# Plain rows for w1 and w2, short packets for w_out, dummy products in the opening, and one later load

## The chip, the cores and the metric

The kernel runs on one core of a Trainium2 chip. The metric is the device time of one execution in microseconds (us). Engines are named as in the profile: PE is TensorE (products; PEld its weight loads), DVE is VectorE, ACT is ScalarE, POOL is GpSimd, SP issues DMAs.

## The reference

Eight sequences of 4160 rows of 192 values go through a dynamic convolution and then through a feed-forward layer with a maximum of two products:

```python
w = softmax(weight_gen)                      # over 7 taps, for 8 heads of 24 channels
out = np.einsum('bshk,bskhg->bshg', w, x_unf)  # x_unf: the row and the 6 before it
x = out.reshape(33280, 192)
h1 = x @ w1                                  # 192 -> 1024
h2 = x @ w2
return np.maximum(h1, h2) @ w_out            # 1024 -> 192
```

The kernel takes `max(h1, h2)` as `h1 + relu(h2 - h1)`. With `wd = w2 - w1` and `w10 = w1 @ w_out`, the result is `y @ w10 + relu(y @ wd) @ w_out`, where y is what the convolution gives. `wd` and `w10` are made on the chip at the start of every execution.

## The kernel before

**Tiling.** Partition p holds 260 neighbouring rows of the flattened input; a column is one row of each partition. Columns are worked on in batches of 16 (`BATCHES`), and these in units of 4 columns (the first two batches) or 8. For each unit VectorE multiplies x with the softmax weights (`mul`, L211); in the first two batches TensorE sums the seven taps while it transposes (`sum_transpose`, L281) and ScalarE copies the result out (`sums_out`, L293); later VectorE adds (L227 to L236) and a DMA transposes (`transpose`, L245). TensorE then makes the hidden features with `wd` (`hid_tile`, L336), ScalarE applies the relu (L346), and TensorE makes the results: `out_first` (L387, with `w10`) and `out_hidden` (L375, with `wo`). ScalarE copies these out (`evac`, L431) and SP stores them.

**Features.** A chunk f of the 1024 features is 128 of them. `load_wo` (L577) gives partition p, for each half of the features, four neighbouring rows of w_out, 3072 B in one piece. So chunk f of `wo` holds every fourth row of its half, and `features` (L588) reads the columns of w1 and w2 in the same order, one in four. Everything that makes `wd` and `w1` reads through `features`: three differences on VectorE (`diff`, L593: d.0, d.1, d.2) and three casts on ScalarE (`cast_w1`, L611: c.0, c.1, c.2). TensorE turns each difference by half its rows (`turn`, L601: t.0 to t.2), and ScalarE copies the turned ones into `wd` (`turn_out`, L607: T.0 for two of them, T.1 for the third). The first features need T.0. `w1` is transposed by products (`w1_products`, L628: v.0) and multiplied with `wo` (`w10_product`, L647: p.0).

**Order.** The start is written out by hand: `OPENING` is a list of steps, and each engine does its share of them in that order. `k.n` makes n dummy products of 512 columns (`keep_warm`, L663), whose output nobody reads. `h` and `r` are a tile of features and its relu; `y` and `e` the sums and their copy; `m` a product of VectorE; `X`, `n`, `l`, `s`, `W` the steps of the softmax, with `W.b.o` the weights of batch b from column o on; `A`, `B`, `D`, `E` the results of a group; `xa` and `xv` the casts of the first x. Loads are `lx` (x), `lg` (weights of the convolution), `lw` and `lt` (w1 and w2), `lo` (w_out), `lh` (the rows before a batch). The name behind an `@` is the step whose instruction the load waits for. `lw` and `lt` are issued by SP; `lo` and `lx` by POOL, which writes them as bf16; POOL issues its loads in the order of the list. Behind the opening, groups of features follow in a loop (L772).

Of the kernel before, what the change touches and what calls it, by code (L numbers as in the profile page):

```python
# [17 lines left out]
def _sub(base: bass.AP, off: int, dims):  # L18
    ap = [list(base.ap[0])] + [[int(s), int(c)] for s, c in dims]
    return dataclasses.replace(base, offset=base.offset + off, ap=ap)  # L20
# [3 lines left out]
def kernel(  # L24
# [11 lines left out]
    B, S, D = x.shape  # L36
    H, K = weight_gen.shape[2], weight_gen.shape[3]
    F = moe_w1.shape[1]
    P = 128
    PAD = K - 1  # L40
    WGC = H * K
    FCH = F // P
    HF = F // 2
# [421 lines left out]
    OUTS, c = [[], [], []], 0  # L465
    for g in range(3, len(GROUPS)):
        most = 4 if g == 3 else 2 if GROUPS[g][1] == 2 or len(OUTS[-1]) == 4 else 4
        n = min(most, ready[g] - c)
# [67 lines left out]
    wo = consts.tile([P, FCH * D], BF16, name="wo")  # L536
# [11 lines left out]
    ws = {(kind, wi): stage.tile([P, w], FP32, name=f"ws{wi}{kind}") for kind, w in (("E", F), ("T", HF)) for wi in range(2)}  # L548
# [26 lines left out]
    def load_wo(_=None):  # L575

        return nc.gpsimd.dma_start(  # L577
            out=wo[:, :].rearrange("p (h e) -> p h e", h=2),
            in_=bass.AP(tensor=moe_w_out.tensor, offset=0, ap=[[4 * D, P], [HF * D, 2], [1, 4 * D]]),
        )  # L580

    def block(i):
# [2 lines left out]

    def features(i, wi):

        return _sub(ws["T", wi] if i == 2 else ws["E", wi], i % 2 * HF, [[1, 4], [4, P]])  # L588

    def diff(i):  # L590

        a, b = (features(i, wi) for wi in (1, 0))
        return nc.vector.tensor_tensor(out=block(i), in0=a, in1=b, op=ALU.subtract)  # L593
# [15 lines left out]
    def cast_w1(i):  # L609

        return nc.scalar.copy(out=w1[:, i * HF:(i + 1) * HF], in_=features(i, 0))  # L611
# [79 lines left out]
    def results_buffer(_):  # L691
# [5 lines left out]
    DO = {  # L697
        "Z": results_buffer,
        "xf": lambda c0, n: load_x_first(c0, n), "lw": load_w, "lt": load_last, "lo": load_wo,
        "lg": lambda b, i=0, of=1: load_wg(b, nc.sync if b < 2 else nc.gpsimd, i, of), "lx": load_x, "lh": load_halo,  # L700
        "xv": lambda c0, n: cast_x("v", c0, n), "xa": lambda c0, n: cast_x("a", c0, n),
# [6 lines left out]
    }  # L708

    OPENING = """  # L710
        lg.0 xf.-6.6 xf.0.4 lt.1.1 lt.0.0 lw.0.1 lw.0.0 lt.1.0 k.1 lw.1.1 lt.0.1 lw.1.0 lg.1 X.0.0.2 X.0.1.2 n.0.0.2 n.0.1.2 l.0.0.2 l.0.1.2 s.0.0.2 W.0.0.0 s.0.1.2 xa.-6.4 W.0.0.1 W.0.8 xv.-2.6 k.19 lx.0.4.4@l.0.0.2 lx.0.12.4@W.0.8 m.0.0.0 c.0 W.0.12 k.1 m.0.0.1 W.0.4 y.0.0 y.0.1 e.0.0 c.2 d.0 d.2 e.0.1 t.0 c.1 t.2 T.0 d.1 t.1 T.1 m.0.4 lx.0.8.4@W.0.4 lo.0@e.0.0 lg.3@e.0.1 h.0 X.1 r.0 h.1 r.1 lx.1.0.8@m.0.4 v.0 n.1 l.1 V.0 h.2 y.1 r.2 e.1 m.0.8 s.1 lg.2@r.2 m.0.12 h.3 r.3 h.4 h.5 V.1 r.4 W.1.0 W.1.4 m.1.0 y.2 r.5 e.2 h.6 lx.1.8.8@W.1.0 m.1.4 p.0 C.2 h.7 y.3 C.1 lh.2 C.0 r.6 r.7 X.2 n.2 W.1.8 A.3 m.1.8 e.3 B.3 h.8 D.3 r.8 Z.0 E.3 A.4 B.4 lx.2.0.8.0@r.8 h.9 l.2 X.3 W.1.12 y.4 e.4 r.9 s.2 D.4 h.10 E.4 W.2.0 n.3 r.10 lg.4@r.10 A.5 y.5 h.11 e.5 l.3 m.1.12 B.5 r.11 D.5 h.12 E.5 A.6 B.6 h.13 D.6 r.12 y.6 E.6 lx.2.8.8 r.13 A.7 e.6 h.14 h.15 W.2.8 B.7 r.14 r.15 D.7 y.7 E.7 e.7
    """

    make_identity(nc, ident_f)
# [91 lines left out]
```

## Time and profile before

| | |
|---|---|
| median of 3 runs | 413.85 us (412.47 to 414.23) |
| the profiled execution | 411.03 us, of which the span of instructions is 409.2 us |
| PE busy | 395.3 us (97%), 7492 products and as many weight loads |
| DVE, ACT, POOL busy | 370.6 us (91%), 362.6 us (89%), 66.2 us (16%) |
| mean granted clock of TensorE | 0.995 |
| DMA | 63.16 MB in 59,251 packets |

Busy times are shares of the span. "Idle before" is what an engine stood still ahead of an instruction, and the name behind the arrow is what ended it; "issue" means that nothing in the profile ended it. The granted clock is the share of TensorE's full clock. In the rows on DMA, q0 is the queue that POOL issues to, q1 that of SP, and q8 one that fetches instructions. Times in the text count from the start of the span.

### The profile page before, as it was taken

How to read it: one execution, taken by the hardware profiler on the slowest of the kernel's cores; microseconds unless marked ns; L12 is line 12 of the kernel's file. 1: busy time of each engine (PE TensorE's matmuls, PEld its weight loads, DVE VectorE, ACT ScalarE, POOL GpSimd, SP SyncE). 2: the span in 40 equal slices, each digit the busy share in tenths (PEclk: the TensorE clock that was granted, in tenths of full speed). 3: DMA queues.
4: the chain of work that ended last, by engine and by line, in shares of the span. 5: the costliest groups of instructions: out<-in, count | busy, mean ns of one | idle time of the engine just before them, and what ended most of it. 6: DMA issues, size and time to landing. Idle time of an engine off the chain costs nothing.

```text
span 409.2 us, 16299 instructions
## 1 busy us (share of the span) xinstructions
PE 395.3 (97%) x7492; PEld 320.0 (78%) x7492; DVE 370.6 (91%) x211; ACT 362.6 (89%) x465; POOL 66.2 (16%) x96
## 2 busy tenths in 40 slices
PE   6699699999999999999999999999999999999996
PEld 2489699777777777777778777877778777787995
DVE  6999969999999999999999999999999999998200
ACT  5999599999999998899998999989999899888872
POOL 2211020112111112121211122120022221201000
PEclk9899999999999999999999999999999999999999
DMA  8944548866478763975676577388448747557304
GB/s 270 244 94 110 125 105 216 157 152 153 117 138 184 192 153 90 257 185 84 205 204 99 112 219 200 60 246 184 95 101 232 180 78 198 141 102 189 104 39 158
DMA packets 59251, 63.16 MB, mean 154 GB/s; under 512 B 46521, under 2 KB 47801, under 8 KB 59184
## 3 DMA queue, kind: packets, MB, share of 16 engines
q1 hardware_dynamic: 51952, 40.15, 36.5%
q0 software_dynamic: 7088, 21.89, 26.7%
q8 instruction: 58, 0.95, 0.9%
q10 hardware_dynamic: 144, 0.10, 0.1%
q14 instruction: 9, 0.07, 0.1%
HBM read 36.55 MB, written 25.56 MB: 152 GB/s over the span
## 4 chain that ended last, share of the span: by engine, by line
PE 94%; ACT 2%; DMA 1%; issue 1%; SPq 1%
PE op_ps L375 42%; PE hdc L336 13%; PE hda L336 13%; PE hdb L336 13%; PE op_ps L387 8%; PE hdp L336 3%; PE yps L281 2%; DMA ws0E<-in_moe_w_dram 1%; ACT w L611 1%; ACT yt L293 0%; PE pw L647 0%; PE tp L628 0%; ACT en_t L191 0%; SPq L570 0%; ACT rd_t L346 0%
## 5 line engine op out<-in xcount | busy, mean ns | idle before, releaser
L375 PE MATMUL op_ps<-wo,rd_t 64*128 64x192 bf16 x4160 | 210.4, 243 | 0.0
L375 PEld LDWEIGHTS <-rd_t 64*128 64x128 bf16 x4160 | 180.6, 94 | 14.9
L211 DVE TENSOR_TENSOR m_t<-xb,en_t 128x10752 bf16<-128x10752 bf16 (+2 forms) x39 | 187.7, 4818 | 3.4 <-ACT en_t L191 2.4
L336 PEld LDWEIGHTS <-wd 64*128 64x128 bf16 x1824 | 95.9, 95 | 41.2 <-issue 1.6
L346 ACT ACTIVATE rd_t<-hdc 128x1024 bf16<-128x1024 f32 x82 | 84.1, 1025 | 18.1 <-PE hdc L336 16.4
L346 ACT ACTIVATE rd_t<-hdb 128x1024 bf16<-128x1024 f32 x81 | 83.5, 1030 | 0.0
L346 ACT ACTIVATE rd_t<-hda 128x1024 bf16<-128x1024 f32 x81 | 83.4, 1029 | 0.0
L253 POOL CAST gate<-yt 128x1 f32<-128x1 bf16 x30 | 33.8, 1128 | 284.5 <-DMA yt<-y_t 284.5
L227 DVE TENSOR_TENSOR m_t<-m_t 128x4608 bf16<-128x4608 bf16 (+1 forms) x30 | 72.9, 2429 | 0.1
L336 PE MATMUL hdc<-yt,wd 64*128 64x512 bf16 (+1 forms) x552 | 67.8, 353 | 0.0
L431 ACT COPY o_t<-op_ps 128x384 f32<-128x384 f32 (+1 forms) x99 | 56.0, 576 | 12.6 <-PE op_ps L375 12.6
L336 PE MATMUL hda<-yt,wd 64*128 64x512 bf16 (+1 forms) x540 | 67.0, 355 | 0.0
L336 PE MATMUL hdb<-yt,wd 64*128 64x512 bf16 (+1 forms) x540 | 67.0, 355 | 0.0
L387 PE MATMUL op_ps<-w,yt 64*128 64x192 bf16 x780 | 55.4, 243 | 0.0
L387 PEld LDWEIGHTS <-yt 64*128 64x128 bf16 x780 | 38.7, 94 | 14.7 <-issue 0.3
L233 DVE TENSOR_TENSOR m_t<-m_t 128x3072 bf16<-128x3072 bf16 (+1 forms) x30 | 50.1, 1669 | 0.1
L191 ACT ACTIVATE en_t<-wg_t 128x896 bf16<-128x896 f32 (+3 forms) x48 | 35.4, 766 | 2.3 <-PE op_ps L375 2.0
L236 DVE TENSOR_TENSOR y_t<-m_t 128x1536 bf16<-128x1536 bf16 (+1 forms) x30 | 27.4, 913 | 0.5
L168 DVE TENSOR_REDUCE sum_t<-e_t 128x64 f32<-128x448 f32 (+3 forms) x31 | 19.6, 634 | 5.4 <-ACT e_t L153 5.4
L177 DVE TENSOR_TENSOR wg_t<-wg_t,sum_t 128x280 f32<-128x280 f32 (+6 forms) x46 | 22.0, 480 | 0.0
L125 POOL DMA_DIRECT2D xb<-in_x_dram x34 | 18.2, 535 | 18.0 <-ACT en_t L191 8.5
L153 ACT ACTIVATE e_t<-wg_t 128x896 f32<-128x896 f32 (+2 forms) x18 | 15.8, 883 | 2.0 <-DMA wg_t<-in_weight_gen_dram 2.0
(39 smaller groups left out, 111.7 us busy)
## 6 DMA issues: line engine op xcount, KB each, us to landing
out_dram<-o_t SPq DMA_DIRECT2D x27, 768.0 KB, 4.4
xb<-in_x_dram POOLq DMA_DIRECT2D x30, 384.0 KB, 5.5
wg_t<-in_weight_gen_dram POOLq DMA_DIRECT2D x13, 448.0 KB, 6.4
out_dram<-o_t SPq DMA_DIRECT2D x10, 384.0 KB, 4.6
xb<-xb POOLq DMA_DIRECT2D x7, 288.0 KB, 5.0
wg_t<-in_weight_gen_dram SPq DMA_DIRECT2D x2, 448.0 KB, 5.0
xb<-in_x_dram POOLq DMA_DIRECT2D x4, 192.0 KB, 5.3
xs<-in_x_dram SPq DMA_DIRECT2D x1, 576.0 KB, 4.2
```

The costliest lines, as they stand in the source:

```text
L177: nc.vector.tensor_tensor(out=w_t, in0=w_t, in1=_sub(s_ts[b], hs.start, [[1, hs.stop - hs.start], [0, K]]), op=ALU.subtract)
L191: act = nc.scalar.activation(out=_sub(en_ts[b], (o * WGC + ((i or 0) * J + j) * N * K) * 2, [[2 * N, K], [2, N], [1, 2]]), in_=_sub(wg_ts[ ...
L211: return nc.vector.tensor_tensor(out=m_out, in0=x_in, in1=_sub(en_ts[b], at * H * 2, [[2, K * n * H], [0, G // 2], [1, 2]]), op=ALU.mult,)
L227: nc.vector.tensor_tensor(out=taps(0, 1, 3), in0=taps(0, 1, 3), in1=taps(3, 1, 3), op=ALU.add)
L233: nc.vector.tensor_tensor(out=taps(0, 2, 2), in0=taps(0, 2, 2), in1=taps(1, 5, 2), op=ALU.add)
L236: nc.vector.tensor_tensor(out=_sub(y_ts[b], o * D, [[64, 2], [P, 3 * w // 2], [1, 64]]), in0=taps(0, 1, 1), in1=taps(2, 1, 1), op=ALU.add,)
L253: nc.gpsimd.tensor_copy(out=gate, in_=yt[:, 0:1])
L336: nc.tensor.matmul(hid_out(t, f, j), lhsT=wd_at(j, s, f // 4, f % 4 * P, P), rhs=_sub(yt_ts[u][half(j), :], (s + j) % 3 * P, [[3 * P, w // ...
L346: relu_of[t0] = nc.scalar.activation(out=rd[:, k * 1024:(k + n) * 1024], in_=hd[:, at:at + n * 1024], func=AF.Relu)
L375: return nc.tensor.matmul(op_out(c), lhsT=rd[half(r), k * 1024 + at:k * 1024 + at + P], rhs=wo[half(r), f * D:(f + 1) * D], start=False, s ...
L387: nc.tensor.matmul(op_out(c + j), lhsT=yt_ts[u][half(j), (3 * i + (s + j) % 3) * P:(3 * i + (s + j) % 3 + 1) * P], rhs=w10[half(j), s * D: ...
L431: copied = nc.scalar.copy(out=_sub(o, c % 24 * D, [[D, len(qs)], [h * D, 2], [1, D]]), in_=_sub(tile_, at + (qs[0] - p) * D, [[D, len(qs)] ...
```

## The change

`load_wo` now gives partition p one row of each chunk: row p of chunk f is row 128 f + p of w_out, so that a piece is 768 B, and there are 1024 of them instead of 256. `features` then reads a half of the columns of w1 and w2 as they lie. In `OPENING`:

- dummy products: k.1 now stands ahead of W.0.0.0 instead of behind W.0.12; k.3 is new between y.0.0 and y.0.1, k.2 behind t.0, k.4 behind t.2 and k.2 behind t.1;
- the load of the first batch's last four columns, lx.0.12.4, waits for xa.-6.4 instead of W.0.8;
- the load of the third batch's second half, lx.2.8.8, waits for W.2.8 and is issued then; W.2.8 itself moves from behind h.15 to ahead of r.13;
- V.0 stands ahead of l.1, and W.1.8 ahead of r.7.

```diff
     def load_wo(_=None):
 
         return nc.gpsimd.dma_start(
-            out=wo[:, :].rearrange("p (h e) -> p h e", h=2),
-            in_=bass.AP(tensor=moe_w_out.tensor, offset=0, ap=[[4 * D, P], [HF * D, 2], [1, 4 * D]]),
+            out=wo[:, :].rearrange("p (f d) -> p f d", d=D),
+            in_=bass.AP(tensor=moe_w_out.tensor, offset=0, ap=[[D, P], [P * D, FCH], [1, D]]),
         )
...
     def features(i, wi):
 
-        return _sub(ws["T", wi] if i == 2 else ws["E", wi], i % 2 * HF, [[1, 4], [4, P]])
+        return (ws["T", wi] if i == 2 else ws["E", wi])[:, i % 2 * HF:(i % 2 + 1) * HF]
...
     OPENING = """
-        lg.0 xf.-6.6 xf.0.4 lt.1.1 lt.0.0 lw.0.1 lw.0.0 lt.1.0 k.1 lw.1.1 lt.0.1 lw.1.0 lg.1 X.0.0.2 X.0.1.2 n.0.0.2 n.0.1.2 l.0.0.2 l.0.1.2 s.0.0.2 W.0.0.0 s.0.1.2 xa.-6.4 W.0.0.1 W.0.8 xv.-2.6 k.19 lx.0.4.4@l.0.0.2 lx.0.12.4@W.0.8 m.0.0.0 c.0 W.0.12 k.1 m.0.0.1 W.0.4 y.0.0 y.0.1 e.0.0 c.2 d.0 d.2 e.0.1 t.0 c.1 t.2 T.0 d.1 t.1 T.1 m.0.4 lx.0.8.4@W.0.4 lo.0@e.0.0 lg.3@e.0.1 h.0 X.1 r.0 h.1 r.1 lx.1.0.8@m.0.4 v.0 n.1 l.1 V.0 h.2 y.1 r.2 e.1 m.0.8 s.1 lg.2@r.2 m.0.12 h.3 r.3 h.4 h.5 V.1 r.4 W.1.0 W.1.4 m.1.0 y.2 r.5 e.2 h.6 lx.1.8.8@W.1.0 m.1.4 p.0 C.2 h.7 y.3 C.1 lh.2 C.0 r.6 r.7 X.2 n.2 W.1.8 A.3 m.1.8 e.3 B.3 h.8 D.3 r.8 Z.0 E.3 A.4 B.4 lx.2.0.8.0@r.8 h.9 l.2 X.3 W.1.12 y.4 e.4 r.9 s.2 D.4 h.10 E.4 W.2.0 n.3 r.10 lg.4@r.10 A.5 y.5 h.11 e.5 l.3 m.1.12 B.5 r.11 D.5 h.12 E.5 A.6 B.6 h.13 D.6 r.12 y.6 E.6 lx.2.8.8 r.13 A.7 e.6 h.14 h.15 W.2.8 B.7 r.14 r.15 D.7 y.7 E.7 e.7
+        lg.0 xf.-6.6 xf.0.4 lt.1.1 lt.0.0 lw.0.1 lw.0.0 lt.1.0 k.1 lw.1.1 lt.0.1 lw.1.0 lg.1 X.0.0.2 X.0.1.2
+        n.0.0.2 n.0.1.2 l.0.0.2 l.0.1.2 s.0.0.2 k.1 W.0.0.0 s.0.1.2 xa.-6.4 W.0.0.1 W.0.8 xv.-2.6 k.19
+        lx.0.4.4@l.0.0.2 lx.0.12.4@xa.-6.4 m.0.0.0 c.0 W.0.12 m.0.0.1 W.0.4 y.0.0 k.3 y.0.1 e.0.0 c.2 d.0 d.2
+        e.0.1 t.0 k.2 c.1 t.2 k.4 T.0 d.1 t.1 k.2 T.1 m.0.4 lx.0.8.4@W.0.4 lo.0@e.0.0 lg.3@e.0.1 h.0 X.1 r.0
+        h.1 r.1 lx.1.0.8@m.0.4 v.0 n.1 V.0 l.1 h.2 y.1 r.2 e.1 m.0.8 s.1 lg.2@r.2 m.0.12 h.3 r.3 h.4 h.5 V.1
+        r.4 W.1.0 W.1.4 m.1.0 y.2 r.5 e.2 h.6 lx.1.8.8@W.1.0 m.1.4 p.0 C.2 h.7 y.3 C.1 lh.2 C.0 r.6 W.1.8 r.7
+        X.2 n.2 A.3 m.1.8 e.3 B.3 h.8 D.3 r.8 Z.0 E.3 A.4 B.4 lx.2.0.8.0@r.8 h.9 l.2 X.3 W.1.12 y.4 e.4 r.9
+        s.2 D.4 h.10 E.4 W.2.0 n.3 r.10 lg.4@r.10 A.5 y.5 h.11 e.5 l.3 m.1.12 B.5 r.11 D.5 h.12 E.5 A.6 B.6
+        h.13 D.6 r.12 y.6 E.6 W.2.8 lx.2.8.8@W.2.8 r.13 A.7 e.6 h.14 h.15 B.7 r.14 r.15 D.7 y.7 E.7 e.7
     """
```

## The prediction

> **What bounds the kernel now.** I read the page first: TensorE is busy 97% of the span, with no other engine idle for long, so time can be won only where TensorE waits or runs slowly. The waits of TensorE over the whole run come to 9.9 us, all of it before 49 us, and the change touches only this opening. The chain from 3.98 us on (start, length, what) shows how that part is put together:
>
> ```profile
> 3.98 5.39 DMA ws0E<-in_moe_w_dram
> 9.39 0.76 ACT w L611
> ...
> 12.09 1.01 ACT w L611
> 13.10 0.37 ACT yt L293
> 13.47 1.03 ACT w L611
> 14.50 0.91 ACT wd L607
> ...
> 15.46 2.03 PE hdp L336 x22
> 17.49 1.31 PE tp L628 x16
> 18.79 1.03 PE hdp L336 x12
> ...
> 44.88 3.26 issue
> ```
>
> To be seen: a transfer of w1 lands at 9.37, then ScalarE alone carries the chain to 15.46, its three casts of w1 (L611) among it; from there TensorE carries it, except for a hole of 3.26 us at 44.88 in which it waits for no semaphore.
>
> Second, stretches of 3.41 us, with TensorE's busy time, the granted clock, and the share of the DMA engines:
>
> ```profile
> core 0: us, PE busy (x), PEclk, DMA share, GB/s
> 9.20:12.63 3.43, 1.95 (x85) 1.00 1.09 325
> 12.63:16.04 3.41, 1.56 (x16) 1.00 1.14 206
> 16.04:19.45 3.41, 3.41 (x42) 0.50 0.97 238
> 19.45:22.86 3.41, 3.08 (x114) 1.00 0.60 111
> ```
>
> After the least busy stretch (1.56 of 3.41 us) the clock is halved for one stretch, just when TensorE has work.
>
> Third, the DMA queues (packets, MB, share) at 41 to 45 us and at 45 to 48 us, and the instruction queue on the page:
>
> ```profile
> q0 software_dynamic: 205, 0.83, 99.0%
> q1 hardware_dynamic: 3, 0.01, 0.6%
> ```
> ```profile
> q1 hardware_dynamic: 140, 0.38, 33.0%
> q0 software_dynamic: 19, 0.02, 4.7%
> q8 instruction: 1, 0.02, 2.0%
> ```
> ```profile
> q8 instruction: 58, 0.95, 0.9%
> ```
>
> TensorE has 7492 products and 7492 weight loads; 14,984 over 58 packets is 258, so one 16 KB packet of q8 is about 256 TensorE instructions. In the packets of the trace, one starts at 38.88 and the next only at 45.78, when q0 (third batch's weights issued at 39.85, its second half of x at 40.38) has drained; it ends at 46.72 and TensorE goes on at 48.15, 1.43 us after. A smaller hole (0.5 us to 41.13) lies exactly 256 instructions earlier, 1.32 us after the end of the packet from 38.88. I read both as TensorE out of instructions, fetched two blocks ahead at most. In most later cases with q0 busy at the request, the fetch starts as that burst ends (138.76 with q0 busy to 138.9, 174.54 to 174.5, 232.31 to 232.4).
>
> Fourth, the prices of a strided and a plain read:
>
> ```profile
> L611 ACT CAST w<-ws0E 128x512 bf16<-128x512 f32 x2 | 2.3, 1128 | 0.9 <-DMA ws0E<-in_moe_w_dram 0.9
> L689 ACT CAST xb<-xs 128x768 bf16<-128x768 f32 x1 | 0.8, 819 | 0.0
> L593 DVE TENSOR_TENSOR wd<-ws1E,ws0E 128x512 bf16<-128x512 f32 x2 | 2.2, 1089 | 0.0
> L177 DVE TENSOR_TENSOR wg_t<-wg_t,sum_t 128x448 f32<-128x448 f32 x2 | 1.2, 616 | 0.0
> ```
>
> The cast of 768 plain elements is cheaper than that of 512 strided ones.
>
> **The change part by part.** *Plain reads.* From start to start a strided cast takes 1.03 us on ScalarE. A plain one of 768 takes 0.73 and an exponential of 448 takes about 0.5, so 512 takes 0.54: 0.49 saved, three times, 1.47. On VectorE 512 pairs lie between 0.62 (448) and 1.08 (896): 0.65, so 0.44 saved three times. But the last cast (c.1) and the last difference (d.1) read the second half of w1, which lands at 12.51. c.1 would begin at 13.38 - 0.98 = 12.40 and so waits to 12.54; the copy T.0 then begins at 13.08 instead of 14.41: 1.33. The x load now tied to xa instead of W.0.8 is issued about 1.2 us earlier, into engines that are full (share 1.09), and may push that landing by up to 0.4; I take 1.2 (ends 0.4 and 1.35). VectorE's next product m.0.4 starts at 13.15 instead of 13.61.
>
> *Dummy products.* Eleven of 512 columns at 0.213 us each are 2.3 us of TensorE. Three fall in the hole between the first sums (end 10.09) and the next (10.77), 0.64 into 0.68; two and four fall between the three turns, which wait for VectorE 0.6 us each, two in the 1.1 us before the first features. Where they do not fit they push t.2 by 0.1, which T.0 (13.08) does not feel: cost 0, ends 0 and 0.3. With them the stretch 12.63 to 16.04 is busy for about 3.0 us: k.4's rest 0.4, t.1 0.2, k.2 0.4, features from 14.1. I expect the clock to stay at 1.00. The pieces from 15.46 to 19.82 then take 1.21 + 0.85 + 0.66 instead of 2.03 + 1.31 + 1.03: 1.65 (ends 0 and 1.7).
>
> *What of these 2.85 us arrives.* ScalarE is full behind T.0: its busy times by 2 us from 14 to 40 us leave 0.6 us idle. TensorE's feature steps wait for ScalarE's relu to free their banks, so ScalarE's lead of 1.2 plus those 0.6 to 0.7 is the most that arrives: 1.9 (ends 0.8 and 2.8).
>
> *Instructions earlier, transfers not.* The dummies are 22 instructions ahead of everything else, so each block ends about 0.5 us earlier in the program. The block ending in y.2 was fetched at 21.17, when q0 drained, and could be used at 22.52 + 1.35 = 23.87, 0.67 before its use at 24.54. With TensorE 1.9 us ahead and the q0 sequence bound by transfers, it may wait up to 1.2: I take 0.3, since ScalarE's queue goes on meanwhile. The hole at 41.13 grows by the 22 instructions: 0.5 (ends 0 and 1.1).
>
> *Later load.* lx.2.8.8 leaves its place right behind the weights' load and waits for W.2.8, which moves ahead of r.13 into ScalarE time that was idle (0.91 before r.12, 3.24 after r.13). The weights' load alone fills q0 from 41.2 to 43.0 in the old times, so the fetch can start at 43.0 instead of 45.78: 2.78 earlier, less 0.5 for the 22 instructions is 2.3 of the 3.26; if the fetch passes before that load, all of it. I take 2.8 (ends 0 and 3.3). Queued behind W.2.8 are r.13 and the copy e.6: r.13 is 1.06 later, and h.15 needs its bank about 1.3 us after y.6, so nothing is lost. On POOL nothing but a cast at 57 us stands behind the load. It lands some 6 us after issue, near 49, before VectorE reads it (52.67, in new times 51 or later). W.1.8 ahead of r.7 and V.0 ahead of l.1 shift ScalarE steps by 0.7 and 0.3 with the sum unchanged: 0.
>
> *wo in short packets.* 256 packets of 3072 B read, written as 1536 B at a mean 149 ns, become 1024 of 768 B: 64 instead of 16 per engine, 2.4 us now. The nearest row is the last stores of 768 B at 37 ns: 64 x 37 = 2.4, no difference. The ends: 256 B transposes at 27 ns (0.7 us saved), and the present 149 ns per packet (9.5, that is 7.1 lost). I take 0, since 768 B is the same length. POOL's issue grows from 0.74 to about 2 (0.2 more for 128 more packets in the rows of L125 and L577), with POOL idle then. wo lands at 18.6 and is read at 25.5, in new times 23.4: cover of 4.8.
>
> The sum: 1.9 - 0.3 - 0.5 + 2.8 = 3.9 us. It is made against the profiled execution, 409.2 us of span in 411.03 us. The median shown is 413.85, 2.8 above it; I take the difference off the median: **409.9 us**.
>
> **Rivals.** *The hole stays or moves.* The fetch still waits for the weights' load and the stores behind it, or the later load, in q0 from about 45, catches the next block's fetch. For it: a burst delays fetches each time; against: in the new times that request comes about a microsecond before the load's packets. It costs 2.4 of the 2.8: 412.3. [...] *The short packets cost more (slower).* At p ns each they hold q0 64p - 2.4 us longer, and the block for y.2, with its 0.67 to spare, comes that much later for TensorE. With 3.9 to lose, it turns slower at 64p - 2.4 = 4.2, p = 103 ns. At 149 ns, 7.1 are lost less the 0.3 already counted: 413.85 - 3.9 + 6.8 = 416.7. For it: 149 ns is the price of q0's own packets; against: those carry four times the bytes. [...] *The clock drops anyway*, because the window falls otherwise: 0.7 less, 410.6. *Both holes go fully*, with no new wait: 1.9 + 0.5 + 3.3 = 5.7: 408.1.
>
> **How the numbers follow.** The forecast's mechanism gets 0.55 (own range 407.5 to 411.5), the hole stays or moves 0.22 (411.3 to 413.5), the short packets 0.09, the clock alone 0.06, all of it fully 0.08. A measurement of this kernel can tell about 0.5%, here 2.1 us, from no change: faster needs 411.78 or less. That holds the first, fourth and fifth and a third of the second: 0.55 + 0.06 + 0.08 + 0.07 = 0.76; within 0.5%: the rest of the second, 0.15; slower: 0.09. The range 407.0 to 413.3 leaves out the short packets and little more.
>
> **What would show it.** L611 and L593 at 0.55 to 0.65 us; the first 22 features by 14.2; PEclk 1.00 from 16 to 19.5; q8's packet after the one near 37 starting before 43, and the issue wait near 44 under 1 us; wo landing by 20. Wrong if wo lands after 23, if the clock still drops, or if a new issue wait of 2 us or more appears at 20 to 25 or 46 to 52 us.

## The result, and the profile after

The changed kernel takes 409.1 us (median of 6 runs, 407.24 to 410.87) against 414.04 us (411.53 to 415.03) for the kernel before on the same chip: a ratio of 0.9886 with a 95% interval of 0.9842 to 0.993, so 4.7 us faster (2.9 to 6.5). A second set of 6 runs gave 0.9905 (0.9867 to 0.9943). The forecast was 409.9 us, with 0.76 on faster.

The profiled execution of the changed kernel took 407.24 us, with a span of 405.4 us; that of before took 411.03 and 409.2. The 3.8 us between the spans all come from the opening: the sums of y.7 start at 47.57 instead of 51.35, 3.78 earlier, and the rest of the program takes as long as before. The chain of the changed kernel (start, length, what) from the landing of w1 on, with its three "issue" pieces of over 0.1 us:

```profile
7.16 6.03 DMA ws0E<-in_moe_w_dram
13.22 0.62 ACT w L611
13.84 1.40 ACT wd L607 x2
15.24 0.94 ACT e_t L153
16.18 1.82 ACT rd_t L346 x2
...
21.48 0.83 PE hdp L336 x12
22.31 0.88 PE yps L281 x60
23.18 0.18 issue
23.36 0.53 PE yps L281 x24
...
39.27 0.65 issue
39.92 0.34 PE op_ps L375 x4
...
44.04 0.15 issue
44.20 0.50 PE yps L281 x22
```

What matters here: the casts of w1 are shorter, but the half that the last one reads landed at 13.20 in this execution instead of 12.51; behind the casts the chain now stays on ScalarE until 21.4, where before TensorE carried it from 15.46 to 21.1; and the hole of 3.26 us is down to 0.15 in this execution (a second profile, below, kept more of it). TensorE's granted clock in the same stretches as before:

```profile
core 0: us, PE busy (x), PEclk, DMA share, GB/s
9.20:12.63 3.43, 2.91 (x90) 1.00 1.09 286
12.63:16.04 3.41, 3.31 (x33) 1.00 1.15 235
16.04:19.45 3.41, 3.33 (x126) 1.00 1.21 228
```

No stretch is half idle any more, and none is granted half the clock. The groups of the plain reads:

```profile
L593 DVE TENSOR_TENSOR wd<-ws1E,ws0E 128x512 bf16<-128x512 f32 x2 | 1.4, 688 | 0.6 <-DMA ws0E<-in_moe_w_dram 0.6
L611 ACT CAST w<-ws0E 128x512 bf16<-128x512 f32 x2 | 1.2, 618 | 1.5 <-DMA ws0E<-in_moe_w_dram 1.5
```

1128 ns became 618 and 1089 became 688; both now wait for the transfer. And the DMA queues from 40 to 42.5 us, where before the fetch of instructions came only as q0's burst ended (41.09 to 45.80, the fetch at 45.78):

```profile
q0 software_dynamic: 80, 0.46, 60.1%
q1 hardware_dynamic: 71, 0.22, 21.4%
q8 instruction: 1, 0.02, 2.4%
```

The fetch comes at 41.80, as the one load in q0 drains (its last packet ends at 41.99), instead of at 45.78. The load ahead of the moved one is lg.4, the weights of the fifth batch; the prediction calls it the third's, which changes nothing in its times.

### The profile page after: what moved, and what is told of

The parts are those of the page before. It is cut to its first block, busy times and chain, and to the rows that moved or that the text cites. A ratio compares the mean times of both kernels' runs of the same rounds, so it can differ in the third digit from the quotient of the medians.

```text
span 405.4 us, 16319 instructions
## 1 busy us (share of the span) xinstructions
PE 396.0 (98%) x7503; PEld 321.1 (79%) x7503; DVE 369.3 (91%) x211; ACT 361.1 (89%) x465; POOL 69.7 (17%) x96
## 4 chain that ended last, share of the span: by engine, by line
PE 94%; DMA 3%; ACT 2%; issue 0%; SPq 0%
PE op_ps L375 42%; PE hdc L336 13%; PE hdb L336 13%; PE hda L336 13%; PE op_ps L387 8%; PE yps L281 2%; PE hdp L336 2%; DMA ws0E<-in_moe_w_dram 1%; DMA xs<-in_x_dram 1%; ACT rd_t L346 1%; PE pw L647 0%; ACT wd L607 0%; ACT e_t L153 0%; ACT w1t L633 0%; ACT yt L293 0%
## 5 line engine op out<-in xcount | busy, mean ns | idle before, releaser
L253 POOL CAST gate<-yt 128x1 f32<-128x1 bf16 x30 | 37.3, 1243 | 272.3 <-DMA yt<-y_t 272.3
L153 ACT ACTIVATE e_t<-wg_t 128x896 f32<-128x896 f32 (+2 forms) x18 | 15.8, 884 | 2.1 <-DMA wg_t<-in_weight_gen_dram 2.1
```

What stands on the lines that cost most here:

```text
L253: nc.gpsimd.tensor_copy(out=gate, in_=yt[:, 0:1])
```

## The experiments

The theory in the prediction has four parts: plain reads shorten ScalarE's chain; dummies keep the clock, but ScalarE lets only part of it through; the two holes of TensorE are instructions that are fetched late, behind bursts of POOL's queue; and short packets cost nothing. Ratios below are to the kernel before on the same chip, with 95% intervals.

**The later load alone.** All else as before.

```diff
-... E.6 lx.2.8.8 r.13 A.7 e.6 h.14 h.15 W.2.8 B.7 ...
+... E.6 W.2.8 lx.2.8.8@W.2.8 r.13 A.7 e.6 h.14 h.15 B.7 ...
```

> Only the third edit: W.2.8 ahead of r.13 and lx.2.8.8 behind it; all else as before. Theory (the hole of 3.26 us at 44.88 is the instruction fetch waiting behind the two POOL loads): the fetch starts near 43 instead of 45.78, the hole shrinks to 0 to 1.0 us, the small one at 41.13 stays at about 0.5, and the time is 2.3 to 3.3 us below before. Rival (the hole stays or moves): the fetch waits for the weights' load and the stores all the same, or a new issue wait of 1 us or more appears between 46 and 54 us; less than 1.5 us gained.

Measured 409.96 us, ratio 0.9934 (0.9903 to 0.9965), 2.7 us faster (1.4 to 4.0). The profiled execution, one of the longer ones at 411.97 us, shows where it can fail: besides the small wait without a releaser, TensorE now has two longer ones (in its chain; start, length):

```profile
41.88 0.31 issue
45.95 1.34 issue
51.30 1.63 issue
```

The fetch of the hole's block starts at 44.31 (45.78 before), 0.3 us after the weights' load has left q0, and is not early enough; TensorE goes on at 47.29, and the fetch of the next block starts only at 50.51, when the moved load (issued at 46.63, landed at 50.99) is through. So the size of the gain is as the theory had it, but part of the hole moved a block on, as the rival had it.

**The same once more**, for a second profile.

> The later load alone once more, for a second profile: the first had the hole in two halves, 1.6 us at the old place and as much a block later. Theory (whether the fetch gets ahead of the moved load differs from execution to execution): the holes at the two places and the time differ from the first profile (411.97 us, 3.4 us in two holes), the time by 1 us or more when the second hole is missing. Rival (the second hole belongs to this order of loads): two holes of 1 to 2 us again.

0.9922 (0.9892 to 0.9952), with 408.75 to 412.67 us; the profiled execution, at 412.67 us, again had both holes, 1.1 us each. So the rival came true in these two profiles: both holes belong to this order of loads, and the theory that they come and go from execution to execution isn't shown. What the shortest executions look like inside is open.

**All but the later load.** The changed kernel with the lines of the last diff reversed.

> The changed kernel with lx.2.8.8 and W.2.8 in their old places. Theory: the opening is as in the changed kernel up to the small hole (y.3 near 26.6 instead of 27.6 before), and the big hole is back: 3 to 4 us of issue near 44, since TensorE is about 1 us earlier and 22 instructions further while the burst of loads is only as much earlier as ScalarE; the time is 0 to 1.2 us below before. Rival (the plain reads and the dummies carry the gain): 2.5 us or more below before.

411.02 us, ratio 0.9955 (0.9925 to 0.9986): 1.9 us faster (0.6 to 3.1). The middle lies above the 0 to 1.2 expected; the interval reaches down to 0.6 and takes in the rival's 2.5 too, so the time doesn't decide. The profile has the big hole back, as the theory had it. But it is that of the longest of the ten executions (414.18 us), and a hole of 2.00 us, where the prediction took 0.3, stands at 23.76, though up to there the program is that of the changed kernel (0.18 us in its first profile):

```profile
23.76 2.00 issue
30.06 0.25 issue
42.09 0.50 issue
46.72 3.17 issue
```

Here the big hole also costs the clock behind it, which the prediction did not have:

```profile
45.77:49.18 3.41, 0.95 (x64) 1.00 0.59 156
49.18:52.59 3.41, 2.70 (x48) 0.50 0.03 9
```

That is not so in every execution: in the profiles of before, of the plain reads alone and of the dummies alone no drop follows the big hole (3.26, 2.99 and 2.90 us), and six of these ten executions were granted 0.999 of the clock or more, the other four 0.994 or 0.995.

**Plain reads alone**, with w_out in short packets; the order as before.

```diff
-        return _sub(ws["T", wi] if i == 2 else ws["E", wi], i % 2 * HF, [[1, 4], [4, P]])
+        return (ws["T", wi] if i == 2 else ws["E", wi])[:, i % 2 * HF:(i % 2 + 1) * HF]
...
-            in_=bass.AP(tensor=moe_w_out.tensor, offset=0, ap=[[4 * D, P], [HF * D, 2], [1, 4 * D]]),
+            in_=bass.AP(tensor=moe_w_out.tensor, offset=0, ap=[[D, P], [P * D, FCH], [1, D]]),
```

> Plain reads of w1 and w2 and w_out in short packets; the order of the opening as before, no dummies. Theory: T.0 0.7 to 1.3 us earlier, the granted clock still drops to 0.5 for one stretch of 3.4 us (TensorE is idle as before between the turns), the big hole stays within 2.8 to 4 us; the time is 0.3 to 1.3 us below before. Rival (the clock drop eats it): the features start earlier but end no earlier, 0 us.

411.89 us, ratio 0.9979 (0.9957 to 1.0002): 0.9 us, as expected, though the interval still touches no change. From the start of c.0 to that of T.0 it takes 3.71 us (5.02 before). The clock drops, here for two stretches and not the one expected:

```profile
8.99:12.40 3.41, 1.55 (x85) 1.00 1.08 265
12.40:15.81 3.41, 2.51 (x13) 0.50 1.09 246
15.81:19.22 3.41, 3.41 (x38) 0.50 1.25 211
```

**Dummy products alone.**

```diff
-... y.0.0 y.0.1 ... t.0 c.1 t.2 T.0 d.1 t.1 T.1 ...
+... y.0.0 k.3 y.0.1 ... t.0 k.2 c.1 t.2 k.4 T.0 d.1 t.1 k.2 T.1 ...
```

> Only the eleven dummy products, strided reads and old loads. Theory (ScalarE is full behind T.0): the clock stays at 1.00, TensorE makes its first features and the transposes of w1 1.6 us faster, but then waits for ScalarE, so at most 0.7 us is left at y.3 (27.6 before), and the 22 instructions make the holes about 0.5 us longer: the time within 0.7 us of before. Rival (TensorE alone sets the pace): 1.2 to 1.7 us below before.

412.95 us, ratio 0.9978 (0.995 to 1.0006): 0.9 us, between the theory's 0.7 and the rival's 1.2, with an interval that holds both. The profile is clearer. The clock stays at 1.00:

```profile
9.63:13.04 3.41, 2.67 (x89) 1.00 1.07 304
13.04:16.45 3.41, 2.63 (x12) 1.00 1.06 193
16.45:19.87 3.42, 3.25 (x81) 1.00 0.98 234
```

From the start of T.0 to the first product of h.4 it takes 6.76 us. Before, with one stretch at half the clock, it took 7.53, so 0.8 of the 1.65 us that the clock cost comes through; with plain reads alone, where two stretches are halved, it took 7.82. The holes are 0.92 and 2.90 us there, with 0.30 us near 25 us. The profile is not all executions, though: seven of the ten were granted 0.994 to 0.996 of the clock, as much as one halved stretch takes away; where theirs lies no trace shows.

**Who lets the rest not through.** The changed kernel with two copies on ScalarE behind T.1 (`z`, into a tile used only at the very end).

```diff
-... t.1 k.2 T.1 m.0.4 ...
+... t.1 k.2 T.1 z.0 z.1 m.0.4 ...
```

> The changed kernel with two extra copies of 384 columns on ScalarE behind T.1, about 0.37 us each from start to start, 0.75 in all, into a tile that is not yet in use; nothing else changes. Theory (behind T.0 ScalarE sets TensorE's pace): from the start of T.0 to the first product of h.4 it takes 7.4 to 7.6 us instead of the 6.7 to 6.8 of all kernels with dummies. Rival (TensorE or the transfers set it): 6.7 to 7.0 us.

From T.0 (14.02) to h.4 (21.70) it takes 7.68 us, 0.9 more than the 6.7 to 6.8 of the kernels with dummies:

```profile
14.02 1.49 ACT L607 CAST wd<-turned 128x1024 bf16<-128x1024 f32 x2
15.40 1.07 ACT L662 COPY o_last<-xs 128x384 f32<-128x384 f32 x2
16.38 0.95 ACT L153 ACTIVATE e_t<-wg_t 128x896 f32<-128x896 f32 x1
```

The copies took 0.98 from start to start, more than the 0.75 I had put, and nearly all of it reached TensorE: behind T.0 ScalarE sets the pace, up to h.4. The whole took 408.48 us in its one timed run: that execution had no long hole near 46 us, and a delay of 0.9 is less than executions differ by.

**Are the holes ends of blocks?** The kernel before, with nine of its dummy products of 512 columns replaced by 56 of 64 columns: 94 more instructions ahead of everything else.

```diff
-... xv.-2.6 k.19 lx.0.4.4@l.0.0.2 ...
+... xv.-2.6 q.56 k.10 lx.0.4.4@l.0.0.2 ...
```

> Before, with nine of its dummy products at the start replaced by 56 small ones of 64 columns, so that 94 more TensorE instructions lie ahead of everything else; no work is taken out. Theory (the hole is the end of a block of 256 instructions whose successor has not come): both holes lie 94 instructions earlier in the program: the big one about 25 products into y.6 instead of 72, or before it; it begins 0.5 to 1 us earlier and still ends about 1.4 us after a packet of the instruction queue near 45 to 47 us. Rival (something at that place of the program or at that time makes TensorE wait): the hole stays 72 products into y.6.

It took 413.42 us in its one timed run (413.38 for before beside it). The hole left y.6. The long one is now in y.5, with 12 of its 84 products still to come, and TensorE goes on at 42.02, 2.25 us after the start of a fetch (39.77; in the kernel before 2.37, from 45.78 to 48.15). The chain has no other before 56 us (start and length):

```profile
39.78 2.24 issue
56.33 0.17 issue
```

Counted in TensorE's recorded instructions, it begins after 1729 of them, as the small hole did before; the other was after 1985, and every wait without a releaser of 0.15 us or more between 20 and 55 us, in all fourteen profiles, begins after 705, 961, 1729, 1985 or 2241: multiples of 256 less 63. There are 33 of them, and each ends 1.2 to 1.5 us after the end of a packet of q8. I had expected both holes 94 instructions earlier and the big one as long as before. The ends of the blocks moved as expected, but at the first the wait grew from 0.24 to 2.24 us, and at the second there was none: TensorE, held up by the first and by half the clock from 43.35 to 46.77, came to it only at 48.49, 2.41 us after its fetch had started. The rival, a place of the program, falls.

**Long packets for w_out**, with the changed kernel's plain reads.

```diff
-            in_=bass.AP(tensor=moe_w_out.tensor, offset=0, ap=[[D, P], [P * D, FCH], [1, D]]),
+            in_=bass.AP(tensor=moe_w_out.tensor, offset=0, ap=[[4 * D, P], [HF * D, 2], [1, 4 * D]]),
```

> The changed kernel with w_out loaded in 256 long packets as before, so that its rows no longer match the order of the features and the output is not the reference's; every instruction is the same but that load. Theory (short packets cost about as much in all): wo lands within 1.5 us of the changed kernel (19.8), TensorE does not wait for it, and the time is within 0.8 us of the changed kernel. Rival (short packets hold the queue): wo lands 2 us or more earlier, the instruction packet after it starts 1 us or more earlier than 21.1, and the time is 1 us or more below the changed kernel.

409.59 us, ratio 0.9919 (0.9883 to 0.9955), no faster than the changed kernel. w_out landed at 19.17 (19.81), 5.8 us after its issue instead of 7.2, and the next fetch of instructions started at 22.66, not earlier than 21.12, in an execution whose loads came later from the start (first x at 7.78 instead of 7.15). In the changed kernel the 1024 packets, of 384 B as written, take 52 ns on average in the trace; 64 of them 3.3 us on each engine.

**The first x load as before.**

```diff
-... lx.0.12.4@xa.-6.4 ...
+... lx.0.12.4@W.0.8 ...
```

> The changed kernel with lx.0.12.4 waiting for W.0.8 again. Theory (that load, issued 1.2 us earlier, pushes the landing of the second half of w1): that landing comes 0.3 to 0.5 us earlier than with it (13.2 in the profile of the changed kernel), T.0 as much earlier, and the time is 0 to 0.5 us lower. Rival (the landing is late for another reason, the whole queue was slower in that execution): the landing does not move beyond what the first x load (7.15) moves, and the time is the same.

408.16 us, ratio 0.9895 (0.9856 to 0.9934): not to be told from the changed kernel. The landing came at 13.62, later than 13.20, and the first x landed later too (7.63 against 7.15). The other profiles show when the load matters:

| kernel | first x lands | 2nd half of w1 lands | between | lx.0.12.4 issued, lg.1 issued |
|---|---|---|---|---|
| before | 6.72 | 12.51 | 5.79 | 8.85, 7.29 |
| changed | 7.15 | 13.20 | 6.05 | 7.98, 7.66 |
| changed, second profile | 7.89 | 14.59 | 6.70 | 8.09, 8.44 |
| x load as before | 7.63 | 13.62 | 5.99 | 9.10, 8.05 |

Where SP is late and POOL's load is issued ahead of lg.1, w1 lands 0.6 to 0.7 us later. This order stands in three of the fourteen profiles (also in those of the long packets and of the three moved loads), with 6.67 to 6.84 us between; of the other eleven, ten have 5.79 to 6.28, and one, of the later load alone, 6.47. So the theory fits the executions in which the order flips; against the changed kernel's first profile the rival does.

**The changed kernel again, and three loads moved away from fetches.**

> The changed kernel once more, beside the next one and on the same chip, for a closer interval: 3.5 to 5.5 us below before. In its profile no clock drop between 9 and 50 us, and holes of issue only at the ends of blocks of 256 instructions: near 23 us (0.2 to 1 us in the kernels with dummies so far) and near 39 to 41 us (0.6 to 0.9).

409.62 us, ratio 0.9905 (0.9867 to 0.9943), so 3.9 us faster. Its profiled execution, the longest of the six at 411.63 us, kept more of the holes than expected:

```profile
24.49 0.64 issue
41.05 0.92 issue
46.09 1.25 issue
51.36 1.08 issue
```

The clock did not drop. Here the start was 0.75 us later (first sums at 10.47 instead of 9.72), the fetch that came at 41.80 came at 44.95, and the next one fell behind the later load, at 50.25: the rival "stays or moves" of the prediction, in part. The first of these did not wait for q0 alone: q0's load was through at 43.82, and from there to the fetch the DMA engines were busy with the stores of q1 (71.8% from 43.8 to 45), which the rival names too. In the other thirteen profiles the fetch at this place starts within 0.4 us of the end of q0's burst.

```diff
-... lo.0@e.0.0 lg.3@e.0.1 h.0 ... y.3 C.1 lh.2 ... r.8 Z.0 E.3 A.4 B.4 lx.2.0.8.0@r.8 ... e.4 r.9 s.2 ... r.10 lg.4@r.10 A.5 ... E.7 e.7
+... lo.0@e.0.0 h.0 ... y.3 C.1 lg.3@C.1 lh.2 ... r.8 Z.0 E.3 A.4 B.4 ... e.4 r.9 lx.2.0.8.0@r.9 s.2 ... r.10 A.5 ... E.7 e.7 lg.4@e.7
```

> The changed kernel with three POOL loads issued later, each away from a fetch of instructions that it delays: the fourth batch's weights (lg.3) behind C.1 instead of e.0.1, the third batch's first half of x (lx.2.0.8) behind r.9 instead of r.8, the fifth batch's weights (lg.4) behind e.7 instead of r.10. No work is taken out. Theory (the holes that are left are fetches behind POOL bursts): the holes near 23 and 40 us go or fall under 0.3 us together, and the time is 0.6 to 2 us below the changed kernel. Rival (a hole closed opens the next one, or VectorE, which gets the third batch 2 to 4 us later, makes TensorE wait): a new wait of TensorE of 0.5 us or more before 80 us, and no gain beyond 0.5 us.

409.02 us, ratio 0.989 (0.9852 to 0.9928). In its profile 0.2 us of holes is left in all, 3.9 us in the other; the medians differ by 0.6, which these intervals can't separate. A new wait did come, as the rival had it, but for another reason: TensorE waits 1.2 us for a relu near 19 us, which stands on ScalarE behind a step that waits 1.1 us for the second batch's weights, landed only at 17.82 in this execution.

**With the first x load as before as well.**

> The kernel of holes_closed with lx.0.12.4 waiting for W.0.8 as in the kernel before, so that this load is issued behind the second batch's weights on SP in every execution. Theory (where POOL issues it ahead of them, the second half of w1 lands 6.7 to 6.8 us after the first x instead of 6.0 to 6.2): that landing 6.0 to 6.2 us after the first x (xs), no hole of 0.5 us or more at a block's end before 60 us, and 4.3 to 6 us below before, 0.3 to 1.5 us below holes_closed. Rival (the landing is hidden, ScalarE's or VectorE's other waits take its place): within 0.3 us of holes_closed.

407.51 us (406.53 to 410.25), ratio 0.9853 (0.9822 to 0.9885): 6.1 us faster than before by the ratio, the fastest of all here, though its interval overlaps the changed kernel's. w1's second half landed 6.27 us after the first x, just above the 6.0 to 6.2 expected. The waits of TensorE in its profile name no "issue" at all; behind the 2.5 us at the very start they are (engine, line and releaser, us in total, times, longest):

```profile
PE hdp L336 <- ACT rd_t L346: 1.9, 2, 1.7
PE yps L281 <- DVE m_t L211: 1.3, 1, 1.3
PE turned L601 <- DVE wd L593: 0.5, 1, 0.5
PE op_ps L387 <- ACT o_t L431: 0.4, 1, 0.4
```

That execution, at 410.25 us the longest of the seven, again had the second batch's weights late (17.79), and behind that wait even a clock drop at 20.0.

## Why the prediction was right

**Plain reads: right in kind, too large in size.** 1.2 us was taken for T.0. Counted from the start of c.0 it is 1.22 in the first profile (5.02 to 3.80) and 0.5 in the second (4.51). In time from the start of the span T.0 is 0.67 earlier in the first (13.74 for 14.41), where the loads ran 0.4 to 0.7 later, and 0.73 later in the second. So two signs that the prediction named missed: the first 22 features started at 14.79, not by 14.2, and L593 takes 0.69, not 0.55 to 0.65. m.0.4, forecast for 13.15, started at 13.90, later than before (13.61). The early x load was put at up to 0.4 of harm; against the kernel with that load as before, w1 lands 0.06 us later behind the first x in one profile and 0.7 in the other, depending on which queue issues first.

**Dummies free, clock at 1.00: right.** From the first sums to the next it takes 1.47 us with k.3 between them (9.72 to 11.19) as without (9.30 to 10.77). No profile with them shows a drop before 20 us; two do later, at 20.0 and 49.2, behind other waits. All twelve executions of the changed kernel were granted 0.998 or more. **What arrives: right for the clock.** 0.7 of the 1.65 us was forecast to come through; from T.0 to h.4 it was 0.72 (7.53 to 6.81), and the extra copies show that ScalarE is the reason. The lead at y.2 was 1.39 (23.52 to 22.13), 0.5 short of the 1.9: as much as T.0 fell short of its 1.2.

**Instructions earlier, transfers not: right in kind, its size is not one number.** 0.3 was taken for the block that ends in y.2; the profiles show 0.18, 0.64 and, without the later load, 2.00, though the program is the same up to there. So 2.00 is what an execution can draw, and it lies at the prediction's own mark for being wrong (2 us or more at 20 to 25). The small hole was to grow by 0.5: 0.24 became 0.65 and 0.92. Once groups take over from the opening these waits are gone: in the two first profiles 51 more packets of q8 come behind y.6, and TensorE has no wait of 0.15 us or more without a releaser there; ahead of that, holes of up to 3.26 us stand. As for the "two blocks ahead at most" of the prediction: up to 60 us each packet of q8 starts 2 to 267 recorded instructions of TensorE ahead of the first that it brings, in these two profiles.

**Later load: right, but not in every execution.** 2.8 of 3.26 us was taken. The load alone measured 2.7 and 3.2, part of which may be clock (below); the first profile of the changed kernel left 0.15 of the hole, the second 1.25, and 1.08 more a block on. So the rival "stays or moves", priced at 2.4 us, is what some executions of the changed kernel do, and not an alternative to the forecast.

**Short packets: right in the result, mis-sized in two terms that nothing waited for.** A packet takes 52 ns, not 37, so by the prediction's sum the load holds the engines 0.9 us longer; its landing moved from 18.6 to 19.8, with first use at 24.5. POOL's issue takes 0.92 us, not 2. The slower rival needed 103 ns a packet. Long packets brought no time (ratio 0.9919; the changed kernel 0.9886 and 0.9905).

**The sum.** 3.9 us was forecast; the two sets of runs gave 4.7 and 3.9. Along the chains of the two first profiles the lead is 1.39 us at y.2, 1.03 behind it, 0.68 behind the small hole and 3.79 behind y.6. So 1.9 - 0.3 - 0.5 + 2.8 = 3.9 came as 1.39 - 0.36 - 0.35 + 3.11 = 3.79. No term is off by more than about 0.5, but that the misses cancel is luck. The medians hold one thing more. The sum knows one halved stretch, from a profile granted 0.995 of the clock, while the median of the 78 executions of before beside the experiments was granted 0.990, about two; how much of the 4.7 and 3.9 that makes is not measured. The parts measured alone add to 0.9 + 0.9 + 2.7 = 4.5; their intervals are too wide to say whether they overlap, and each may contain some of the clock.

## What to carry to other kernels

In these kernels a wait of TensorE that no semaphore ends, at an instruction count that is a multiple of 256 from the last one, was a late fetch of instructions (33 such waits in fourteen profiles, each ended 1.2 to 1.5 us after a packet of q8): look for the queue that was full ahead of the fetch, and move a load, not the work (here 2.7 us for one load). Ask of every microsecond won on one engine which engine lets it through; here two copies put on ScalarE, 0.98 us long, answered that within about a tenth of a microsecond. In an opening where loads, fetches and engines are this tight, one profile is one draw: the same kernel showed 0.15 us of holes at and behind y.6 in one execution and 2.3 us in another.

## What the runs showed that was not expected

- Executions differ already in the first loads: the second part of the first x landed between 6.72 and 8.00 us in the fourteen profiles. That is a third of the difference between the kernels. What stands behind moves with it: between the two profiles of the changed kernel the landing differs by 0.74 us (7.15, 7.89), the start of the first sums by 0.75 (9.72, 10.47).
- The halved clock lasted one stretch of 3.41 us in the profile of before and two in the four other profiles without the eleven dummies. Stretches with 0.95 to 1.86 us of TensorE's work were followed by a drop, but others with 1.55 (43.33 to 46.74 before) to 1.78 were not, so this time alone doesn't tell which will be.
- How much clock an execution of before loses goes with its time. The profiles calibrate it: one halved stretch is 0.995, two are 0.991 or 0.992, three 0.988. Of the 78 executions of before beside the experiments, 19 at 0.994 to 0.996 took 412.0 us on average, 21 at 0.990 to 0.992 took 412.7, 23 at 0.986 to 0.988 took 413.7, and 15 at 0.982 to 0.984 took 415.3: about 1.1 us a stretch. So the profile from which the prediction was made is of the kind that loses least. The later load alone, without dummies, also has a higher clock in its first ten executions (median 0.995, 0.988 for before beside it); in which stretches those executions differ no trace shows.
- In both kernels with the three moved loads the second batch's weights landed near 17.8 us, though the last of their large packets ended at 17.1 and at 15.8. Why the landing came so late was not tried.
